# The last part's rows stored in twelve transfers of 32 rows over two queues instead of three of 128 rows

## The chip, the cores and the metric

One core of a Trainium2 chip. The metric is the device time of one execution in microseconds (us). All runs that are compared here are in the same state, the one the records call fast; only runs 9 to 11, one execution each, are of unknown state. A ratio between two kernels is the mean time of one kernel's fast runs over the mean time of the other's fast runs of the same rounds, so it is not quite the ratio of the medians quoted beside it.

## The reference, cut to what matters

```python
scores = scale * x @ state^T ; a = softmax(scores)   ; xread = a @ state    # 8 x 8 x 512 x 64
scores2 = scale * state @ x^T; a2 = softmax(scores2) ; sread = a2 @ x       # 8 x 8 x  32 x 64
x = concatenate([xread, sread], axis=2)              # per batch 512 + 32 = 544 rows
h = x @ w_in ; g = h * erf(softplus(h)) ; out = g @ w_out                   # (4352, 512), float32
```

Each of the 8 batches owns 544 rows of the output: 512 rows of tokens and then 32 rows of states. The kernel computes the token rows batch by batch. The state rows of all batches, 8 x 32 = 256 rows, come last, as one part of two 128-row tiles, each of them 4 batches x 32 rows. In the output these four groups of 32 rows lie 544 rows apart.

## The kernel before: the parts concerned

The end of every part adds partial products into two output tiles and stores them. `put` is `put_x` for token rows and `put_s` for the last part.

```python
def store7(acc, put):
    ...
    nc.scalar.copy(m1, acc[2][:, 0:E2])                    # E2 = 256 columns
    add(two(o1), twice(m1), two(acc[0]))
    put(0, o1, slice(0, E2))                               # first half of the first tile
    add(u3, c12, acc[2][:, E2:])                           # c12 = o1[:, E2:]
    add(two(o2), twice(u3), two(acc[1]))
    put(1, o2)                                             # second tile, whole rows
    add(c12, c12, acc[1][:, E2:])
    add(c12, c12, acc[3][:, 0:E2])                         # needs the last matmul
    put(0, o1, slice(E2, d_model))                         # last half of the first tile

def put_x(b, h):
    rows = out[TB * b:TB * b + S].rearrange("(c p) e -> c p e", p=P)
    def go(r, ot, c=slice(0, d_model)):
        nc.sync.dma_start(out=rows[2 * h + r][:, c], in_=ot[:, c])
    return go

def put_s(r, ot, c=slice(0, d_model)):
    m = P // Ns                                            # 128 // 32 = 4
    rows = out.rearrange("(b t) e -> b t e", t=TB)[m * r:m * r + m, S:]
    nc.sync.dma_start(out=rows[:, :, c], in_=ot[:, c])     # DRAM side 4 x 32 x columns
```

An access pattern lists its dimensions from the slowest to the fastest. On the DRAM side of `put_s` the slowest has size 4 (the batches), then come 32 rows, then the columns; of `put_x` both sides begin with 128 rows. In the profile's lines SPq is the sync queue and ACTq is ScalarE's queue.

Of the kernel before, what the change touches and what calls it, by code (L numbers as in the profile page):

```python
# [16 lines left out]
def kernel(  # L17
# [17 lines left out]
    nc = tc.nc  # L35
    B, H, S, D = x.shape
    Ns = state.shape[2]
# [8 lines left out]
    TB = S + Ns  # L46
# [45 lines left out]
    for e in range(2):  # L92
        nc.sync.dma_start(out=st[:, 0, D * e:D * e + D],
                          in_=state[0].rearrange("(i e) n d -> e i n d", e=2)[e])
# [435 lines left out]

    def put_s(r, ot, c=slice(0, d_model)):
        m = P // Ns
        rows = out.rearrange("(b t) e -> b t e", t=TB)[m * r:m * r + m, S:]
        nc.sync.dma_start(out=rows[:, :, c], in_=ot[:, c])

    def tiles(n):
        return [ps_o.tile([P, d_model], F32, name="o%d" % r) for r in range(n)]
# [120 lines left out]
    for b in range(1, B + 1):  # L658
        if b < B:
            groups = fast(b, 2, lambda h, b=b: put_x(b, h))  # L660
        else:
            groups = fast(b, 1, lambda h: put_s)
# [63 lines left out]
```

## Time and profile before

| | before |
|---|---|
| time, median of the first 3 runs | 763.88 us (763.88 to 764.07) |
| span of the profiled run | 761.9 us |
| TensorE busy | 741.8 us, 97% |
| end of the last addition | 754.09 us |
| last addition to end of span | 7.8 us |

The last row is the one to keep: the end of the last addition is its start plus its length in the chain of waits (753.67 + 0.42), and 761.9 - 754.09 = 7.8. I call it the tail. It separates what the stores do from whatever happens earlier. The profile's lines for it are in the prediction.

### The profile page before, as it was taken

How to read it: one execution, taken by the hardware profiler on the slowest of the kernel's cores; microseconds unless marked ns; L12 is line 12 of the kernel's file. 1: busy time of each engine (PE TensorE's matmuls, PEld its weight loads, DVE VectorE, ACT ScalarE, POOL GpSimd, SP SyncE). 2: the span in 40 equal slices, each digit the busy share in tenths (PEclk: the TensorE clock that was granted, in tenths of full speed). 3: DMA queues.
4: the chain of work that ended last, by engine and by line, in shares of the span. 5: the costliest groups of instructions: out<-in, count | busy, mean ns of one | idle time of the engine just before them, and what ended most of it. 6: DMA issues, size and time to landing. Idle time of an engine off the chain costs nothing.

```text
span 761.9 us, 12108 instructions
## 1 busy us (share of the span) xinstructions
PE 741.8 (97%) x5076; PEld 595.8 (78%) x5076; DVE 512.7 (67%) x767; ACT 386.8 (51%) x497; POOL 0.7 (0%) x6
## 2 busy tenths in 40 slices
PE   8998999999999999999999999999999999999995
PEld 6533435698888888988888888888898889999994
DVE  3888879856767566947595776756694755684441
ACT  5868864744465544553464446554455344443330
POOL 0000000000000000000000000000000000000000
PEclk9999999999999999999999999999999999999999
DMA  7665752420031201320042003120000000000000
GB/s 225 202 244 202 165 96 70 98 57 28 1 52 43 53 22 17 68 57 28 1 83 57 28 1 51 48 48 22 1 29 2 29 1 28 1 28 1 28 1 29
DMA packets 108587, 42.74 MB, mean 56 GB/s; under 512 B 96116, under 2 KB 99956, under 8 KB 108532
## 3 DMA queue, kind: packets, MB, share of 16 engines
q1 hardware_dynamic: 106420, 41.43, 20.4%
q8 instruction: 40, 0.66, 0.3%
q10 hardware_dynamic: 2112, 0.52, 0.3%
q14 instruction: 15, 0.12, 0.1%
HBM read 33.03 MB, written 8.91 MB: 55 GB/s over the span
## 4 chain that ended last, share of the span: by engine, by line
PE 78%; DVE 10%; ACT 3%; issue 1%; DMA 0%; SPq 0%; DVEq 0%
PE o L503 44%; PE h L397 23%; PE at L326 3%; PE o L453 2%; PE h L439 2%; ACT s L447 1%; DVE hs L405 1%; DVE m L194 1%; PE at L221 1%; DVE z L184 1%; DVE raw L475 1%; DVE xT L295 1%; ACT L447 1%; DVE m L294 1%; DVE s L448 1%
## 5 line engine op out<-in xcount | busy, mean ns | idle before, releaser
L448 DVE TENSOR_TENSOR s<-s,hs 128x2048 f32<-128x2048 f32 x34 | 77.9, 2292 | 74.2 <-ACT s L447 74.1
L404 ACT ACTIVATE s<-hs 128x512 f32<-128x512 f32 x120 | 75.6, 630 | 86.2 <-DVE hs L405 85.9
L503 PE MATMUL o<-w_out,s 128*128 128x256 f32 x480 | 118.3, 380 | 0.0
L503 PE MATMUL o<-raw,hs 128*128 128x256 f32 x480 | 116.3, 385 | 0.0
L503 PE MATMUL o<-w_out,hs 128*128 128x256 f32 x480 | 115.4, 381 | 0.0
L503 PEld LDWEIGHTS o<-raw,hs 128*128 128x128 f32 x480 | 88.4, 190 | 31.4 <-issue 20.1
L503 PEld LDWEIGHTS o<-w_out,hs 128*128 128x128 f32 x480 | 89.8, 190 | 16.3 <-issue 4.2
L405 DVE TENSOR_TENSOR hs<-hs,h 128x512 f32<-128x512 f32 x90 | 61.5, 684 | 49.8 <-PE h L397 49.7
L503 PEld LDWEIGHTS o<-w_out,s 128*128 128x128 f32 x480 | 84.5, 191 | 7.8
L397 PEld LDWEIGHTS h<-aT,m 128*128 128x128 f32 x672 | 84.4, 192 | 6.4 <-issue 1.6
L397 PE MATMUL h<-aT,m 128*128 128x128 f32 x672 | 85.6, 276 | 0.4 <-DVE hs L405 0.4
L405 DVE TENSOR_TENSOR hs<-s,h 128x512 f32<-128x512 f32 x60 | 41.1, 685 | 56.2 <-PE h L397 55.8
L447 ACT ACTIVATE s<-s 128x2048 f32<-128x2048 f32 x34 | 65.0, 1911 | 0.4
L408 ACT COPY s<-h 128x512 f32<-128x512 f32 x30 | 17.5, 582 | 92.4 <-PE h L397 92.4
L453 PE MATMUL o<-w_out,s 128*128 128x512 f32 x128 | 59.1, 600 | 0.9 <-DVE s L448 0.9
L397 PE MATMUL h<-sy,sx 128*128 128x128 f32 x448 | 59.5, 275 | 0.0
L397 PEld LDWEIGHTS h<-sy,sx 128*128 128x128 f32 x448 | 56.7, 192 | 2.2 <-ACT hs L413 0.6
L503 PE MATMUL o<-raw,s 128*128 128x256 f32 x240 | 57.9, 379 | 0.0
L413 ACT COPY hs<-h 128x512 f32<-128x512 f32 x30 | 17.4, 582 | 73.7 <-PE h L397 73.7
L503 PEld LDWEIGHTS o<-raw,s 128*128 128x128 f32 x240 | 43.3, 191 | 4.6
L453 PEld LDWEIGHTS o<-w_out,s 128*128 128x128 f32 x128 | 23.1, 191 | 30.0 <-issue 28.8
L447 ACT ACT_TABLE_LOAD x34 | 43.6, 1283 | 0.6
(112 smaller groups left out, 902.7 us busy)
## 6 DMA issues: line engine op xcount, KB each, us to landing
raw<-in_moe_w_in_dram SPq DMA_DIRECT2D x8, 1024.0 KB, 5.2
raw<-in_moe_w_out_dram SPq DMA_DIRECT2D x8, 1024.0 KB, 4.9
x<-in_x_dram SPq DMA_DIRECT2D x60, 128.0 KB, 2.7
xq<-in_x_dram SPq DMA_DIRECT2D x112, 64.0 KB, 2.1
out_dram<-ot SPq DMA_DIRECT2D x19, 256.0 KB, 2.0
out_dram<-ot SPq DMA_DIRECT2D x30, 128.0 KB, 1.7
x<-in_x_dram ACTq DMA_DIRECT2D x4, 128.0 KB, 4.1
st<-in_state_dram SPq DMA_DIRECT2D x8, 56.0 KB, 4.2
```

The source lines that it names most:

```text
L184: nc.vector.reduce_sum(out=z1, in_=a, axis=AX.X)
L326: nc.tensor.matmul(out=ps[e][q, :], lhsT=stT[b][r, q], rhs=w_in[r, fs, i, :], start=True, stop=True)
L397: last = nc.tensor.matmul(out=bank[:, q], lhsT=lhsT, rhs=rhs, start=(first and i == 0 and k == 0), stop=(i == GF - 1 and k == len(ops) - 1 ...
L404: nc.scalar.activation(out=s[:, k], in_=hs[:, k], func=ACTF.Softplus)
L405: add = lambda o, x, y: nc.vector.tensor_tensor(o, x, y, op=ALU.add)
L408: nc.scalar.copy(m1, p)
L413: nc.scalar.copy(c11, p)
L439: on_pe = nc.tensor.matmul(out=hp, lhsT=m_t[b, f // GF][:, e, P * (f % GF):P * (f % GF) + P], rhs=aT[b][:, e], start=(e == 0), stop=(e == 1))
L447: return (nc.scalar.activation(out=s, in_=s, func=ACTF.Erf), nc.vector.tensor_tensor(s, s, hs, op=ALU.mult))
L448: nc.vector.tensor_tensor(s, s, hs, op=ALU.mult))
L453: nc.tensor.matmul(out=acc[r], lhsT=gT[:, i, P * r:P * r + P], rhs=w_out[:, GF * g + i, :], start=(g == 0 and i == 0), stop=(g == NG - 1 a ...
L503: nc.tensor.matmul(out=acc[bank][:, E2 * c:E2 * c + E2], lhsT=lhs[:, i, :], rhs=rhs[:, g, i, :], start=(first and i == 0 and c == 0), stop ...
```

## The change

Its intent is that each transfer is a plain block of 32 rows, which all the DMA engines can share, and that a second queue helps with issuing the larger number of transfers.

```diff
     def put_s(r, ot, c=slice(0, d_model)):
         m = P // Ns
-        rows = out.rearrange("(b t) e -> b t e", t=TB)[m * r:m * r + m, S:]
-        nc.sync.dma_start(out=rows[:, :, c], in_=ot[:, c])
+        for j in range(m):
+            r0 = TB * (m * r + j) + S
+            queue = nc.scalar if r == 1 or (c.start and j % 2) else nc.sync
+            queue.dma_start(out=out[r0:r0 + Ns, c], in_=ot[Ns * j:Ns * j + Ns, c])
```

## The prediction

> **What bounds the kernel now**
>
> The kernel takes 763.88 us (median of three, 763.88 to 764.07). The change touches only the three stores that write the last 128 x 512 block of results, so I read the page for what bounds the whole, then the chain that ended last, then the last ten microseconds in narrow windows. First the busy tenths of the page, 40 slices of 19 us each:
>
> ```profile
> PE   8998999999999999999999999999999999999995
> DMA  7665752420031201320042003120000000000000
> ```
>
> PE is full in every slice but the last, where it drops to half. The body is bound by TensorE and no store there can matter. The one place where a store can set the end is the last slice. The chain over the last 22 us, in order of time:
>
> ```profile
> 739.82 13.83 PE o L503 x64
> 753.65 0.02 issue
> 753.67 0.42 DVE ot L513
> ```
>
> The last matmul ends at 753.65, the last addition at 753.67 + 0.42 = 754.09, and the span ends at 761.9. So 761.9 - 754.1 = 7.8 us, 1% of the kernel, follow the last computation. What fills them, from the DMA queue's own waits and its timeline (start, length):
>
> ```profile
> SPq L721 <- DMA out_dram<-ot: 5.7, 1, 5.7
> 751.34 0.61 SPq L534 DMA_DIRECT2D out_dram<-ot  x1
> 752.66 0.56 SPq L534 DMA_DIRECT2D out_dram<-ot  x1
> 754.12 0.54 SPq L534 DMA_DIRECT2D out_dram<-ot  x1
> ```
>
> The third store starts its issue at 754.12, 0.03 us after its addition, and ends it at 754.66. Then the sync queue waits 5.7 us for a store to land, to about 754.7 + 5.7 = 760.4, and 1.5 us of closing synchronisation follow. Why a store of 128 KB takes 754.12 to 760.4 = 6.3 us is told by the windows (start:end and length, then five engines' busy time, PE clock, DMA share of 16 engines, GB/s), the first three in the tail and the last two around earlier stores of the same kernel:
>
> ```profile
> 752.50:754.50 2.00, 1.14 (x6) 0.66 (x4) 0.88 (x3) 0.00 (x0) 0.00 (x0) 1.00 0.23 70
> 754.50:755.75 1.25, 0.00 (x0) 0.00 (x0) 0.00 (x0) 0.00 (x0) 0.00 (x0) 1.00 0.24 18
> 755.75:760.00 4.25, 0.00 (x0) 0.00 (x0) 0.00 (x0) 0.00 (x0) 0.00 (x0) 0.86 0.24 85
> ...
> 719.00:719.25 0.25, 0.25 (x5) 0.25 (x4) 0.25 (x2) 0.25 (x1) 0.00 (x0) 1.00 1.05 410
> 720.25:720.50 0.25, 0.25 (x4) 0.25 (x3) 0.00 (x0) 0.00 (x0) 0.00 (x0) 1.00 1.00 352
> ```
>
> In the tail the DMA share stays near 0.25, which is 4 engines of 16, at 85 GB/s and below. The earlier stores, of just the same 128 and 256 KB from the same tiles, reach a share of 1.0 and 352 to 410 GB/s. The page's issues by size give what such an unhampered store costs:
>
> ```profile
> out_dram<-ot SPq DMA_DIRECT2D x19, 256.0 KB, 2.0
> out_dram<-ot SPq DMA_DIRECT2D x30, 128.0 KB, 1.7
> ```
>
> 2.0 and 1.7 us from issue to landing (medians; 16 of the 19 and 28 of the 30 are earlier stores). The three slow ones back up too: 128 + 256 + 128 KB = 512 KB drain in order from about 752.6 to 760.0, so the last, small store stands behind the 256 KB of the second.
>
> **What the Trainium skill says**
>
> "DMA: Bandwidth & Descriptors", section on why a DMA increments its semaphore by 16: the number k of engines is the largest, at most 16, that divides the slowest dimension of both access patterns. The old store's DRAM side is 4 batches x 32 rows x columns, slowest dimension 4; its SBUF side has 128 partitions; so k = 4. The trace agrees, with the share of 0.24 to 0.25. The earlier stores have 128 on both sides, so k = 16, and the trace shows 1.00. The new transfers have 32 rows on both sides, so k should again be 16.
>
> The same page, section "Issuing engines are not separate DMA queues": several issuing engines share the 16 DMA engines and only save issue time. So the second queue is worth issue time, not bandwidth. And "Perfetto Trace Analysis", section "DMA Instruction — HWDGE (DVE, Sync)": the issue slice includes a lock of the descriptor generator for exclusive use. If both queues share that generator, their issues are partly serial. The start of this trace, where both queues issue at once, has 1.37 us for two issues on sync (the first 0.75) beside 2.26 us for four on ScalarE's queue: a little longer than the 0.50 of loads issued alone, which neither proves nor excludes it.
>
> **The change part by part**
>
> Removed: three stores whose issues took 0.61, 0.56 and 0.54 us, on 4 engines. Added: four transfers of 32 KB on sync for the first half of the first tile, four of 64 KB on ScalarE's queue for the second tile, and for the last half four of 32 KB, two on each queue. No computing instruction changes, and ScalarE itself has finished its last copy by 750.22 + 0.37 = 750.59, so its queue is free.
>
> One issue: the earlier plain stores took 0.33 to 0.36 us (min and median of 46), the loads of 32-partition tiles 0.31 at the least, and the four issued by ScalarE's queue at the start 0.42 to 0.64 (those carry four times as many short pieces). I take 0.35 for sync and 0.40 for ScalarE's queue, as estimates.
>
> First half: ready at 751.31, four sync issues from 751.34 to 751.34 + 4 x 0.35 = 752.74. Nothing waits for them; they land by about 754 and are off the path.
>
> Second tile: its addition ends at 751.95 + 0.69 = 752.64; four issues on ScalarE's queue run from 752.66 to 752.66 + 4 x 0.40 = 754.26. With 0.56 each it would be 754.90.
>
> Last half: ready at 754.09. Sync, free since 752.74, issues from 754.12 and starts its second at 754.12 + 0.35 = 754.47. ScalarE's queue is held by the second tile until 754.26, so its second starts at 754.26 + 0.40 = 754.66. That one ends the kernel. By then the data of the second tile is almost through: at the earlier stores' rate of about 390 GB/s, 64 KB take 0.17 us, less than one issue, so no backlog forms.
>
> Landing: 1.7 us for 128 KB, of which 128 KB / 390 GB/s = 0.34 us is data; with 32 KB some 0.25 us less, so 1.45. I take 1.6 for the sharing of the engines and the generator. Landed: 754.66 + 1.6 = 756.3, in place of 760.4. That is 4.1 us less. Of it, the data rate gives most: the 512 KB now never queue. Against it stands the cutting of the last store into two issues per queue, about 0.5 us (754.12 to 754.66).
>
> Afterwards come the same 1.5 us of closing work; waits on twelve completions in place of three are short events of about 0.02 to 0.03 us when already met, at most 0.2 us more. I leave that in the range. Sum: 763.88 - 4.1 = 759.8 us, that is 0.5% less.
>
> **The rivals**
>
> One: the tail is the fixed delay of a write to HBM and not the four engines, so more transfers only add fixed costs. For it: the stretch 754.50 to 755.75 has the four engines busy while moving only 18 GB/s, so something other than raw rate held about 1.2 us. Against it: the 352 to 410 GB/s and 1.7 us of the earlier stores to the same tensor. It would give 763 to 764.5.
>
> Two: the twelve issues become the bound. If ScalarE's issues take 0.56 (as its median at the start) its last starts at 754.90 + 0.56 = 755.46 and lands at 757.1: a saving of 3.3 us, 760.6. If the two queues fully serialise in the generator, the four last issues take 4 x 0.35 = 1.4 us, the last starts at 754.12 + 1.05 = 755.2 and lands near 756.8: 760.3.
>
> Three: 32-row transfers don't get all 16 engines, only 8 say. Then each 32 KB piece takes 0.17 us instead of 0.09, still less than an issue, and the result moves by 0.1 to 0.3 us: 760.
>
> Four: completion semaphores are reused, and a late issue waits for an early transfer. The first is issued at 751.34 and should be down by about 753, well before 754.12, and the queue's waits in the trace list none of the earlier stores waiting for another store. If it happened, 0.5 to 1 us: 760.5.
>
> Five, on the good side: issues of 0.31 us and a landing of 1.4 give 754.12 + 0.31 + 1.4 = 755.8, a saving of 4.6 us: 759.3.
>
> **Range and chances**
>
> Central 759.8. Most rivals lie above it (760 to 760.6), the good case 0.5 below, and a run of the kernel before varies by 0.2, so the range that should hold it 8 times in 10 is 759.2 to 761.0. Faster by 2% would need 15 us, and the whole time after the last computation is only 7.8 us; slower by 2% would need a fault. So the chances are 0.005 faster, 0.99 within 2%, 0.005 slower.
>
> **What would show each step right or wrong**
>
> Up to 754.1 nothing should move: last addition at 754.09 within 0.1 or so. In windows of the tail the DMA share should pass 0.25 well, near 1 in short bursts rather than a plateau, and be back to 0 by about 756.1. The issues should show six on each queue, 0.3 to 0.45 us each; above 0.5 on ScalarE's queue supports rival two. The sync queue's last wait should shrink from 5.7 us to about 1.5 and end near 756.3. If the share stays at 0.25 and the last wait stays above 4 us, the engine count is wrong as a cause. If the share is high but the wait long, rival one holds. If the closing 1.5 us grow beyond 1.8, the number of completions to wait for costs what I took as nothing.

## The result, and the profile after

| | before | after |
|---|---|---|
| runs | 763.88, 763.88, 764.07, 764.02 | 759.74, 759.79, 761.55, 761.68 |
| median | 763.95 us | 760.67 us |
| ratio (95% interval) | | 0.9957 (0.994 to 0.9974) |
| span of the profiled run | 761.9 us | 758.0 us |
| tail | 7.8 us | 4.0 us |

The time fell by 0.4%, which counts as the same at the 2% line, and the median lies inside the predicted range. But the runs fall into two groups 1.9 us apart, which nobody had forecast; the profiled run is of the lower group.

The chain that ended last, in order of time (start, length, what):

```profile
739.95 13.61 PE o L503 x63
753.56 0.02 issue
753.58 0.42 DVE ot L513
```

The computation ends at 753.58 + 0.42 = 754.00, 0.09 us from before. Of the 3.9 us by which the span is shorter, 3.8 lie behind it. The sync queue's last wait (total, times, longest), and from the timeline the last two issues of each queue (start, total length):

```profile
SPq L723 <- DMA out_dram<-ot: 1.6, 1, 1.6
```

```profile
754.03 0.82 SPq L536 DMA_DIRECT2D out_dram<-ot  x2
...
754.47 0.88 ACTq L536 DMA_DIRECT2D out_dram<-ot  x2
```

The wait that lasted 5.7 us lasts 1.6. It starts when the sync queue has issued (754.03 + 0.82 = 754.85) and ends near 756.5; 1.5 us of closing work follow, as before. The new pieces and their time to landing, from the DMA view:

```profile
out_dram<-ot ACTq DMA_DIRECT2D x4, 64.0 KB, 1.7
out_dram<-ot SPq DMA_DIRECT2D x6, 32.0 KB, 1.6
out_dram<-ot ACTq DMA_DIRECT2D x2, 32.0 KB, 1.6
```

And the windows of the tail (last two columns: share of 16 DMA engines, GB/s):

```profile
752.50:753.00 0.50, 0.50 (x4) 0.43 (x3) 0.37 (x2) 0.00 (x0) 0.00 (x0) 1.00 0.24 66
753.50:754.00 0.50, 0.04 (x1) 0.00 (x0) 0.42 (x1) 0.00 (x0) 0.00 (x0) 1.00 0.75 201
755.00:755.50 0.50, 0.00 (x0) 0.00 (x0) 0.00 (x0) 0.00 (x0) 0.00 (x0) 1.00 0.60 191
756.00:756.50 0.50, 0.00 (x0) 0.00 (x0) 0.00 (x0) 0.00 (x0) 0.00 (x0) 0.50 0.06 16
```

The ceiling of 0.25 is gone: the share reaches 0.75, and the transfers are through soon after 756.0 in place of 760.0. The share of 0.24 in the first line is no return of the ceiling: there, 32 KB pieces arrive about every 0.46 us, and 32 KB / 0.46 us is 71 GB/s, close to the 66 of the line. The issues are now what paces the data. The packed traces also keep the completion events of every transfer (`prof` does not print them), and their number agrees with the shares: each store before has one early event and then 4, while each of the twelve pieces after has 16.

### The profile page after: what moved, and what is told of

Read it like the earlier page. It is cut to its first block, busy times and chain, and to the rows that moved or that the text cites. A ratio compares the mean times of both kernels' runs of the same rounds, so it can differ in the third digit from the quotient of the medians.

```text
span 758.0 us, 12118 instructions
## 1 busy us (share of the span) xinstructions
PE 741.9 (98%) x5076; PEld 595.8 (79%) x5076; DVE 512.4 (68%) x767; ACT 386.8 (51%) x497; POOL 0.7 (0%) x6
## 4 chain that ended last, share of the span: by engine, by line
PE 77%; DVE 10%; ACT 3%; issue 2%; DMA 1%; SPq 0%; DVEq 0%
PE o L503 43%; PE h L397 23%; PE at L326 3%; PE o L453 2%; PE h L439 2%; ACT s L447 2%; DVE hs L405 1%; DVE m L194 1%; PE at L221 1%; DVE s L448 1%; DVE z L184 1%; ACT L447 1%; DMA raw<-in_moe_w_in_dram 1%; DVE xT L295 1%; DVE raw L475 1%
```

## The experiments

The times of whole runs carry a scatter of about 2 us (run 1 tells why), so the tails are compared. A tail is the span less the end of the last addition, both from the trace of that run; it comes out of one execution each, and a span is printed to 0.1 us, so differences of 0.1 us mean nothing. The changed kernel was traced twice and gave 4.0 both times.

| kernel | end of last addition | span | tail |
|---|---|---|---|
| before | 754.09 | 761.9 | 7.8 |
| changed | 754.00 | 758.0 | 4.0 |
| 1 changed, again | 754.74 | 758.7 | 4.0 |
| 2 twelve transfers, sync alone | 755.60 | 760.8 | 5.2 |
| 3 six transfers of 64 rows | 755.77 | 768.6 | 12.8 |
| 4 three transfers, rows interleaved | 754.16 | 757.7 | 3.5 |
| 5 three transfers, two queues | 754.60 | 762.2 | 7.6 |
| 6 only the last store cut | 754.53 | 761.7 | 7.2 |
| 7 only the first two cut | 754.45 | 759.2 | 4.7 |
| 8 as 4, last store on two queues | 754.41 | 758.1 | 3.7 |
| 9 second store in column halves | 754.18 | 761.2 | 7.0 |
| 10 first store left out | 755.97 | 763.1 | 7.1 |
| 11 last store left out | 756.21 | 762.2 | 6.0 |

Runs 1 to 4 were on one chip, 5 to 8 on one, 9 to 11 on one, each with runs of the kernel before beside them. The results of 1 to 9 are correct; 10 and 11 leave rows out on purpose and are wrong.

**Run 1: the changed kernel again.** No edit.

> The changed kernel unaltered, five rounds, because its four runs fell into two groups (759.74 and 759.79; 761.55 and 761.68) while the kernel before stays within 0.2 us. Theory: the two groups are a property of the kernel (of the tail or of the start, not yet known) and return here with a gap near 1.9 us. Rival: they were one chip's disturbance; then all runs lie within 0.3 us near 759.8. The trace of either group tells where the 1.9 us are.

Measured: 760.57, 761.39, 761.42, 761.71, 761.71; ratio to before 0.9959 (0.9946 to 0.9971). Four runs lie where the upper group lay and one 0.8 us above the lower, but it is not as the theory had it. The kernel before, which had stayed within 0.2 us, now scattered too: 763.52 to 764.30 in seven runs and 765.22 to 765.70 in four, and beside runs 5 to 8 it went from 763.57 to 766.39 in 35. So the scatter is not the change's own. How often a run falls high does differ: about 14 of all 50 runs of the kernel before, 6 of the 9 of the changed kernel. Whether that is chance is open, but it bears on the totals: the means of whole runs differ by 3.1 to 3.3 us in the two comparisons, the tails by 3.8. The tail of this run is the same 4.0 us as in the first trace.

Where the time of the upper group goes is seen in the traces of runs 2 and 3, which fell in it. Of the upper runs of the kernel before and of the changed kernel no trace was kept; that theirs is the same is inferred from the size of the gap. Windows of run 2 (the column before the last two is the granted TensorE clock):

```profile
64.50:65.00 0.50, 0.50 (x2) 0.19 (x1) 0.50 (x1) 0.50 (x2) 0.00 (x0) 0.96 0.03 12
65.00:65.50 0.50, 0.50 (x2) 0.33 (x1) 0.50 (x1) 0.50 (x2) 0.00 (x0) 0.50 0.00 0
...
68.00:68.50 0.50, 0.50 (x2) 0.08 (x1) 0.50 (x2) 0.48 (x2) 0.00 (x0) 0.63 0.00 0
68.50:69.00 0.50, 0.50 (x3) 0.26 (x2) 0.50 (x1) 0.50 (x1) 0.00 (x0) 1.00 0.00 0
```

The same place in the changed kernel's first trace:

```profile
65.00:67.50 2.50, 2.50 (x7) 1.14 (x6) 2.38 (x3) 2.50 (x4) 0.00 (x0) 1.00 0.00 0
```

In run 2 the clock stands at 0.50 from 65.0 to about 68.4, and 3.4 us at half speed lose 1.7 us, the gap between the groups. The Trainium skill has this on "TensorE: Matmul & The Clock Gate", section "Part 1: The HAM clock gate (the "warmup" mystery)": after an idle window of about 3.4 us TensorE runs at half clock until about 3.4 us of activity have been seen, in a window that runs freely, so that it varies from run to run. The length agrees: about 3.4 us. What starts it does not quite: in run 2 TensorE had been idle for only 2.0 us (62.02 to 64.05) and was already at work again when the clock fell near 65.0, and the changed kernel's first trace has the same idle time without the stretch. Why some runs have the stretch and others do not, no run here settles. The groups also have a smaller scatter inside them: weights arrive later in one trace than in another, so that the matmuls near 56 us start up to 0.8 us later (55.96 in run 2, 56.78 in run 1). That makes most of the 0.8 us by which run 1's traced run, which lacks the stretch, lies above 759.74.

**Run 2: one queue.** From the changed kernel:

```diff
-            queue = nc.scalar if r == 1 or (c.start and j % 2) else nc.sync
-            queue.dma_start(out=out[r0:r0 + Ns, c], ...)
+            nc.sync.dma_start(out=out[r0:r0 + Ns, c], ...)
```

> The same twelve transfers, all on the sync queue. If the second queue is worth only issue time, the last of twelve issues of 0.41 us starts near 755.9 in place of 754.9, lands 1.6 us later, and the kernel takes 760.8 us, 1.0 more than the good group of the changed kernel and 3 less than before. If the second queue itself brings the bandwidth, the time goes back to 763 or more. If the two groups of times come from the use of ScalarE's queue at the end, this kernel shows one group only.

Measured: 761.02, 761.44 and, with the half-clock stretch, 762.53 to 762.92 in five; ratio 0.9972 (0.996 to 0.9984). The tail is 5.2, 1.2 longer than with two queues where 1.0 was expected, and 2.6 shorter than before. So the second queue is worth about a microsecond here, as issue time alone would have it, and is not what brings the bandwidth. It also has both groups, which frees ScalarE's queue of that suspicion. The expectation spoke of the lower group; the median of 762.64 is one of the upper.

**Run 3: more transfers, but with slowest dimension 2.** From the kernel before:

```diff
-        nc.sync.dma_start(out=rows[:, :, c], in_=ot[:, c])
+        for j in range(2):
+            nc.sync.dma_start(out=rows[2 * j:2 * j + 2, :, c],
+                              in_=ot[2 * Ns * j:2 * Ns * j + 2 * Ns, c])
```

> Six transfers of 64 rows, all on sync, each with 2 batches as the slowest dimension of its DRAM side. If the slowest dimension sets the number of engines, these run on 2 of 16, the DMA share of the tail falls to 0.12, 512 KB at some 48 GB/s take 10.9 us in place of about 7.5, and the kernel takes 767 to 768.5 us, slower than before in spite of more and smaller transfers. If more and smaller transfers are what helps, it lies between 760 and 763.9.

Measured: 768.42, 768.62, 769.00, 770.37; ratio 1.006 (1.0044 to 1.0076). Windows of its tail:

```profile
760.00:762.00 2.00, 0.00 (x0) 0.00 (x0) 0.00 (x0) 0.00 (x0) 0.00 (x0) 0.50 0.13 51
762.00:764.00 2.00, 0.00 (x0) 0.00 (x0) 0.00 (x0) 0.00 (x0) 0.00 (x0) 0.50 0.13 50
```

A share of 0.13 is 2 engines of 16, at about 25 GB/s each, the same rate per engine as in the old tail (98 GB/s on 4 at its steadiest). Twice the transfers made the kernel slower, as the theory of the slowest dimension says and no theory of the number of transfers does. The tail of 12.8 us is 5.0 longer than before, somewhat more than the expected 3 to 4.5, and three of the four runs lie above the expected 767 to 768.5. The completion events of each of the six stores number 2, after an early one.

**Run 4: still three transfers on one queue, with slowest dimension 32.** From the kernel before, the rows of a tile in the order (row, batch):

```diff
-    sT = const.tile([P, NK, B, Ns], F32, name="sT")
+    sT = const.tile([P, NK, B // 4, Ns, 4], F32, name="sT")
...
-        nc.scalar.copy(sT[:, :, b, :], ps)
+        nc.scalar.copy(sT[:, :, b // 4, :, b % 4], ps)
...
-            Y = sT.rearrange("p (e k) (r b) n -> p e r k (b n)", e=2, r=2)
+            Y = sT.rearrange("p (e k) r n b -> p e r k (n b)", e=2)
...
-        rows = out.rearrange("(b t) e -> b t e", t=TB)[m * r:m * r + m, S:]
+        rows = out.rearrange("(b t) e -> b t e", t=TB)[m * r:m * r + m, S:].rearrange("b t e -> t b e")
```

> Three transfers of 128 rows on sync as before, but the rows of the last part are kept in the order (row, batch) in place of (batch, row), so that the DRAM side of a store is 32 x 4 x columns with slowest dimension 32. If the slowest dimension alone is the cause, all 16 engines take part, the last store starts at 754.1, lands 1.7 us later, and the kernel takes 759.3 us, a little better than the changed kernel, with three transfers and one queue. If the number of transfers or the second queue matters, it stays at 763.9. The result must be as exact as before, since only the order of columns within a matmul changes.

Measured: 759.52, 759.57, 759.75, 759.87, 759.99; ratio 0.9938 (0.9925 to 0.995). Its last wait, its last issue, and two windows:

```profile
SPq L721 <- DMA out_dram<-ot: 1.5, 1, 1.5
```

```profile
754.19 0.54 SPq L534 DMA_DIRECT2D out_dram<-ot  x1
```

```profile
754.00:754.50 0.50, 0.00 (x0) 0.00 (x0) 0.16 (x1) 0.00 (x0) 0.00 (x0) 1.00 1.05 410
...
755.50:756.00 0.50, 0.00 (x0) 0.00 (x0) 0.00 (x0) 0.00 (x0) 0.00 (x0) 0.81 0.58 199
```

The second tile goes out at a share of 1.05 and 410 GB/s. Number of transfers, queue and bytes are as before; only the shape of the DRAM side changed (and with it the order in which the rows are written), and the tail fell from 7.8 to 3.5 us; each store now has 16 completion events. Together with run 3 that settles the cause. It also beats the changed kernel by 0.4 us of tail: the last store begins at 754.19, at once after the addition, and has landed at 754.19 + 0.54 + 1.5 = 756.2; the changed kernel's last of twelve begins 0.9 us after its addition and gets back about half of that by landing sooner (1.6 us from the start of its issue, against 2.0). The 1.7 us between the medians of runs 1 and 4 are mostly the half-clock stretch, which by their times none of these five runs has and four of run 1's have; whether this kernel avoids it or was lucky is open. My expected 759.3 took 1.7 us to landing, the figure for a two-dimensional store; this three-dimensional one needs 2.0 to 2.1 (its issue alone takes 0.54 us, against 0.33).

**Run 5: the second queue alone.** From the kernel before:

```diff
-        nc.sync.dma_start(out=rows[:, :, c], in_=ot[:, c])
+        (nc.scalar if r == 1 else nc.sync).dma_start(out=rows[:, :, c], in_=ot[:, c])
```

> The three old stores of 128 rows, the middle one on ScalarE's queue: the second queue alone. Read by the time from the end of the last addition to the end of the span, which leaves out the half-clock stretch near 65 us that some runs of every kernel have (7.8 us before, 4.0 in the changed kernel). If the engines are the limit, the queue is worth nothing: the same 512 KB go through the same 4 engines, 7.8 within 0.3, time as before. If a store stood behind another because of the queue's order, the last one overtakes and the time falls by up to 2 us.

Measured: median 764.84 of 20 runs, before 764.24 of 35; ratio 1.0002 (0.9995 to 1.0009). Its last wait and two windows:

```profile
SPq L721 <- DMA out_dram<-ot: 5.8, 1, 5.8
```

```profile
755.00:756.25 1.25, 0.00 (x0) 0.00 (x0) 0.00 (x0) 0.00 (x0) 0.00 (x0) 1.00 0.24 25
756.25:760.50 4.25, 0.00 (x0) 0.00 (x0) 0.00 (x0) 0.00 (x0) 0.00 (x0) 0.54 0.24 83
```

The tail of the old kernel stands there almost unchanged: 4 engines, 83 GB/s, and the last wait at 5.8 us. The last store does not overtake.

**Runs 6 and 7: one part of the change alone.** From the kernel before, only the last half's store cut (run 6), or only the first two stores (run 7, the reverse condition, with the second tile on ScalarE's queue):

```diff
-        nc.sync.dma_start(out=rows[:, :, c], in_=ot[:, c])
+        if not c.start:
+            nc.sync.dma_start(out=rows[:, :, c], in_=ot[:, c])
+        for j in range(m if c.start else 0):
+            queue = nc.scalar if j % 2 else nc.sync
+            queue.dma_start(out=rows[j, :, c], in_=ot[Ns * j:Ns * j + Ns, c])
```

> Only the store of the last half is cut into four of 32 rows, two on each queue; the two larger ones before it keep their 4 engines. If the backlog of those 4 engines is what holds the last store, most of the gain stays away: 384 KB still drain through them until about 758.7 and a quarter of the last pieces waits behind, so 6.8 us from the last addition to the end and about 762.9 us, 1 less than before. If the last store's own rate was the cost, it falls to 4.0 us as in the changed kernel and about 760.

> The reverse: the first two stores are cut as in the changed kernel, the last stays one transfer of 128 rows on 4 engines. No backlog then; the last store starts at once and pays only its own data at 4 engines, 128 KB at 97 GB/s = 1.35 us in place of 0.34. By the backlog theory 4.6 us from the last addition to the end and about 760.5 us, 3.3 less than before. If the last store's own rate was the cost, it stays above 6.5 us.

Measured: run 6 762.93 to 765.12 in 12 runs, ratio 0.9999 (0.999 to 1.0008), tail 7.2. Run 7 760.57, 760.98, 762.45, 762.49, ratio 0.9965 (0.9951 to 0.9979), tail 4.7. First a window of run 6, then one of run 7:

```profile
758.00:759.50 1.50, 0.00 (x0) 0.00 (x0) 0.00 (x0) 0.00 (x0) 0.00 (x0) 0.50 0.20 70
```

```profile
756.50:757.50 1.00, 0.00 (x0) 0.00 (x0) 0.00 (x0) 0.00 (x0) 0.00 (x0) 0.63 0.25 90
```

In run 6 the DMA is still busy at 4 engines' pace 4 us after the last addition, though the store that everything waits for has all 16. Its pieces take 5 us to land in place of 1.6 (DMA view of run 6):

```profile
out_dram<-ot SPq DMA_DIRECT2D x2, 32.0 KB, 5.0
out_dram<-ot ACTq DMA_DIRECT2D x2, 32.0 KB, 5.2
```

A part of each goes through the 4 engines that have the backlog, as the completion events show. The second store's four come at 758.48, 759.01, 759.42 and 759.46. Of the last piece's 16, twelve come from 758.28 to 758.76 and the other four at 759.18, 759.71, 760.14 and 760.17, each about 0.7 us after one of the second store's. The twelve are late too, where the changed kernel's last event comes at 756.50; why, these runs do not tell. The expectation was too good: 0.6 us of tail in place of 1, and nothing in the whole runs, about 8 of which are of the upper group by their times. In run 7 there is no backlog, and the last store pays only its own slowness. Of the 3.8 us that the change gains, 7.8 - 4.7 = 3.1 come from cutting the stores that do not end the kernel, and 0.7 from cutting the one that does.

**Run 8: the interleaved kernel with its last store on both queues.** From run 4:

```diff
-        nc.sync.dma_start(out=rows[:, :, c], in_=ot[:, c])
+        if not c.start:
+            nc.sync.dma_start(out=rows[:, :, c], in_=ot[:, c])
+            return
+        for n, queue in enumerate((nc.sync, nc.scalar)):
+            h = slice(c.start + 128 * n, c.start + 128 * n + 128)
+            queue.dma_start(out=rows[:, :, h], in_=ot[:, h])
```

> The kernel with interleaved rows (3.5 us from the last addition to the end, 759.75 us), with its last store cut by columns into two of 64 KB, one on each queue. Once all 16 engines take part, what remains is a fixed delay of about 1.3 us and 0.34 us of data, and the two issues run beside each other: 3.5 within 0.15 us, the same time. If a store's length still mattered, it gains 0.2 us; if the two queues exclude each other at issue, it loses 0.3 to 0.5 us.

Measured: 759.38 to 760.34 in five runs and 762.37 in one; ratio 0.9946 (0.9933 to 0.9959); tail 3.7. That is 0.1 to 0.2 us more than run 4, which rounding does not separate from the expected 0.15. Once all 16 engines take part, spreading over queues brings nothing.

**Runs 9 to 11: the slow stretch in the old tail.** The old tail has 1.25 us at 18 GB/s that the rate of 4 engines does not explain. From the kernel before, run 9 stores the second tile as two column halves, run 10 leaves out the first store and run 11 the last:

```diff
-        nc.sync.dma_start(out=rows[:, :, c], in_=ot[:, c])
+        for h in ((c,) if r == 0 else (slice(0, 256), slice(256, 512))):   # run 9
+            nc.sync.dma_start(out=rows[:, :, h], in_=ot[:, h])
...
+        if r == 1 or c.start:                                               # run 10
+        if not c.start:                                                     # run 11
+            nc.sync.dma_start(out=rows[:, :, c], in_=ot[:, c])
```

> Asks for the cause of one stretch of the old tail: 1.25 us (754.5 to 755.75) with 4 engines busy at 18 GB/s, at the start of the second store. The second tile is stored as two column halves, so every piece on the way is 1 KB as in the first store; still 4 engines throughout. If the 2 KB pieces are the cause, the stretch is gone and the time from the last addition to the end falls from 7.8 to 6.5 us. If it belongs to the second store's place behind another, it stays, at 7.8 or a little more for the extra issue.

> Wrong on purpose: the first half's store is left out. If the slow stretch needs a store in front of the second, it goes: 384 KB from 753.9 at 97 GB/s end near 758.0 and 5.7 us pass from the last addition to the end. If the second store has it by itself, about 7.0 us.

> Wrong on purpose: the last half's store is left out, and the first two are as before. If the issue of the third store (754.12 to 754.66) is what slows the second's start, the slow stretch goes, and the second's 256 KB end near 757.1, so that 4.9 us pass from the last addition to the end. If not, the stretch stays between 754.5 and 755.75 and 6.2 us pass.

Measured, one execution each, so of unknown state: 762.99, 764.90 and 764.03 us beside 764.12 of the kernel before; the traces of 10 and 11 have the half-clock stretch in them, so only their tails count: 7.0, 7.1 and 6.0. Windows of run 9, where the second tile starts, then the slow place of run 10, then that of run 11:

```profile
754.09:754.59 0.50, 0.00 (x0) 0.00 (x0) 0.10 (x1) 0.00 (x0) 0.00 (x0) 1.00 0.20 68
754.59:755.09 0.50, 0.00 (x0) 0.00 (x0) 0.00 (x0) 0.00 (x0) 0.00 (x0) 1.00 0.24 61
755.09:755.59 0.50, 0.00 (x0) 0.00 (x0) 0.00 (x0) 0.00 (x0) 0.00 (x0) 1.00 0.27 90
```

```profile
756.38:756.88 0.50, 0.00 (x0) 0.00 (x0) 0.00 (x0) 0.00 (x0) 0.00 (x0) 1.00 0.26 12
```

```profile
757.12:757.62 0.50, 0.00 (x0) 0.00 (x0) 0.00 (x0) 0.00 (x0) 0.00 (x0) 1.00 0.20 8
```

With no store in front (run 10) and with none behind (run 11) the stretch stays, at 8 to 12 GB/s; the tails are near the 7.0 and 6.2 expected for that. With pieces of 1 KB in place of 2 KB it is gone, and the tail shrinks by 0.8 us, less than the 1.3 expected; run 9 has one issue more and a short dip of its own (68 and 61 GB/s above), but what took the rest was not tested. So the stretch belongs to the second store itself, to whole rows of 2 KB on 4 engines. It may be the long form of something that 1 KB pieces have too: in the kernel before the first store, too, moves only 29 GB/s from 752.75 to 753.00, and 98 from 753.25. Whether the size of the pieces or the unbroken 64 KB of each batch is what matters inside it, these runs do not tell.

## Why the prediction was right

The predicted 759.8 us stands against a median of 760.67 and a lower group at 759.74 and 759.79. The mechanism was right, and the saving nearly: 4.1 us were predicted, and the tail gave 3.8. That the lower group meets 759.8 within 0.06 us is partly luck, since the sum started from 763.88 while the profiled run before took 763.68, and the last addition came 0.09 us sooner. By its steps:

- *The slowest dimension of the DRAM side sets the number of engines.* Shown from both sides: slowest dimension 2 gives a share of 0.13 (run 3), 4 gives 0.24 to 0.25, 32 in an unchanged number of transfers gives 1.05 (run 4).
- *The small last store stands behind the 256 KB before it.* Shown by runs 6 and 7: 3.1 of the 3.8 us. (Runs 9 to 11 put some of it, 0.8 us in run 9, to the slow start of that 256 KB store and not to its amount.)
- *The second queue is worth issue time only.* Supported by run 5 (nothing by itself) and run 2 (1.2 us of tail where there are twelve issues).
- *One issue costs 0.35 us on sync and 0.40 on ScalarE's queue.* Too low. Two issues took 0.82 on sync and 0.88 on ScalarE's queue, so 0.41 and 0.44 each. ScalarE's last two started at 754.47, where 754.26 was predicted, though the addition ended 0.09 sooner.
- *The last piece lands 1.6 us after its issue starts.* The DMA view has 1.6. The landing near 756.5 came 0.2 later than the predicted 756.3, from the issues.
- *The closing 1.5 us stay.* They did; waiting for twelve completions in place of three cost nothing that shows.
- *The share would be near 1 in short bursts.* It was 0.75 at most in half a microsecond and touches 0.9 in slices of 0.2 us: bursts, because an issue takes longer than the data of a piece. Run 4 has 1.05 for half a microsecond.
- *16 of the 19 stores of 256 KB are earlier ones.* A slip: it is 18 (18 and 28 make the 46 earlier stores). Nothing rests on it.

Of the rivals, the first (a fixed delay and not the engines) falls with run 4, and the slow stretch that spoke for it is the property of one old store (runs 9 to 11). The second, full serialisation of the two queues, falls with the trace after: between 754.47 and 754.85 both queues are issuing, and an issue takes 0.41 to 0.44 us there, hardly more than in run 2, where sync issues alone (median 0.41). ScalarE's issues, feared at 0.56, took 0.38 to 0.44. Issue time still holds 0.9 of the 4.0 us of tail, from the last addition to the start of the last issue. The third, only 8 engines, falls with the 16 completion events of each piece, and the fourth, a late issue that waits for an early transfer, with the sync queue's waits after, which name no transfer before the last wait. The fifth, the good case, did not come: issues took longer than 0.31 us and the landing 1.6.

Beside the issue times, the step that failed is the spread: "a run of the kernel before varies by 0.2". It varies by over 2 us, most likely through the half-clock stretch of TensorE near 65 us, which the first four runs happened not to have. Two of the four runs after, 761.55 and 761.68, lie outside the range of 759.2 to 761.0, very likely for that reason; the median is inside with the help of the other two. That was luck: in run 1 the median of the same kernel is 761.42, and over all nine runs it is 761.42 too, outside the range.

## What to carry to other kernels

Look at the DMA share in the windows around a slow transfer: a plateau at a simple fraction such as 0.25 or 0.13 means that few engines carry it, and then the shape of the access pattern, with its slowest dimension, is the thing to change before cutting or spreading the transfer. Cutting into blocks works, but a layout that keeps one large transfer on all engines was better here by about 0.4 us of tail, in one trace, and needs no second queue. And stores that are not the last one can still set the end, by the backlog they leave in front of it.

## What the Trainium skill lacked or had wrong

- "DMA: Bandwidth & Descriptors", section "Issuing engines are not separate DMA queues": it calls the issue time usually small relative to the DMA itself. For these blocks it is not small: an issue takes 0.41 to 0.44 us, more than their data (64 KB at the 410 GB/s of run 4 take 0.16 us) and about a quarter of the 1.6 to 1.7 us from issue to landing.
- The same page, section "Specifications": a first-byte latency of about 0.6 us for these queues, without saying from when it counts. The first three-dimensional store before was issued from 751.34 to 751.95, and the windows show no byte before 752.50: at least 1.1 us from the start of the issue, which is more, but at least 0.55 us from its end, which agrees. The interleaved kernel's last store took 2.0 us to land, where the two-dimensional ones of its size take 1.7.
- "TensorE: Matmul & The Clock Gate", section "Part 1: The HAM clock gate (the "warmup" mystery)": it names an idle window of about 3.4 us as what brings the half clock. Here it came after 2.0 us of idle time, about 0.9 us after TensorE had resumed (run 2), and only in some runs.
- No page that was consulted has the slow start of whole 2 KB rows on 4 engines: 18 GB/s for 1.25 us before, half-microseconds at 8 to 12 GB/s in runs 10 and 11, and not where the same store goes in 1 KB pieces (run 9, 61 GB/s at the least).
- Not wrong, but worth a number: "DMA: Bandwidth & Descriptors", section "Rules for kernel authors", advises one 128-partition transfer in place of two halves, and in another row of its table warns that an outermost dimension below 16 confines a transfer to that many engines. Here the second decided: a tail of 3.5 us in one piece on 16, 4.0 in blocks on 16, 7.8 in one piece on 4.
